# Moving two sets of transposes in the first group of a fused GFNet and GEGLU backward kernel

## The chip, the cores and the metric

The kernel runs on one core of a Trainium2 chip, in one launch. The metric is the device time of a run in microseconds; the median of several runs is given. A profile, taken by the hardware profiler on one further execution, shows every instruction of the five engines: TensorE (PE in the profile's rows, its weight loads PEld), VectorE (DVE), ScalarE (ACT), GpSimd (POOL) and SyncE (SP, which issues transfers here).

## What is computed

The forward pass mixes two branches with a gate; the kernel computes its output and the gradients of seven inputs. Cut to what matters:

```python
def _A_ref(x, w_r, w_i):                      # spectral branch
    X = rfft2(x) * (w_r + 1j * w_i)
    return irfft2(X, s=(S, D)).astype(bfloat16)

def _B_ref(x, w_gate, w_up, w_down):          # GEGLU branch
    return (gelu(x @ w_gate) * (x @ w_up)) @ w_down

x = A_x
g = sigmoid((x * gate_w).sum(-1, keepdims=True))
out = g * _A_ref(x, ...) + (1 - g) * _B_ref(x, ...)
_out, _vjp = jax.vjp(_f, A_x, A_w_r, A_w_i, B_w_gate, B_w_up, B_w_down, gate_w)
return (out, *_vjp(grad_out))
```

The sequence has S = 2048 rows, D = 576 columns, and the hidden width is 4608; tensors are bfloat16. Both branches take the same x.

## The kernel before

The 2048 rows are 16 tiles of 128 rows. The hidden width is cut into 18 groups of 256 columns (`for g in range(NG)`, L986), and each group is worked in four steps m = 0 to 3 of four row tiles each (L990). A step of the hidden layer consists of

- z, the product of the output gradient dO with the transposed down weights: 16 matmuls over four 128-column chunks (L413) and four over the 64-column tail (L418), written to one PSUM tile that ScalarE reads as da (L441);
- gate|up, the product of x with both other weights, in two halves of eight matmuls (L429), each into a PSUM tile of its own, with four tail matmuls ahead (L422). ScalarE reads each half three times: a copy xb and a copy hu (L450, L451) and a square q (L448);
- the element-wise part. `H_ew1` (L456 to L460) is four VectorE operations on the step's own tiles. `H_ew2` is a sigmoid on ScalarE (L476) and eight VectorE operations (L483 to L491), and it is held back by one step (`held`).

From group 1 on, weight gradients of the group before (L535, L553, L567) and pieces of the Fourier transforms are placed between the steps. After the last group a second phase reads the stored hidden gradients back and forms dx and the forward output (L1202).

The matmuls need x and dO with the model dimension on the partitions. The first group makes these transposed tensors, `xT` and `dOT`, on TensorE while it already works with them. `titems` (L370) yields three items for four row tiles: a first set of 8 transposes (chunks 0 and 1), a second set of 8 (chunks 2 and 3), and a third of 4 (the tails). Each item takes a PSUM tile, fills it with transposes (L378, tails L384) and copies it to `xT` or `dOT` (L385), on ScalarE (`AC`) or VectorE (`VC`) as the caller says.

In the first group the PSUM tiles of these items and of the gate's logits come from one pool, `pg`, with two buffers that are taken in turn. `gate(m + 1)` (L389) forms the logits of the next step's rows with 20 small matmuls (L394) and ScalarE reads them with a sigmoid (L396). `do2` are the three items of dO for step m + 2, copied by ScalarE, ScalarE and VectorE; `x1` are the three items of x for step m + 1, copied by ScalarE (VectorE at m = 0), VectorE and VectorE. Items in `rest` are handed to the next step's `H_mm` (L403), which runs them between z's chunks and z's tails (L414). Items in `early` run before the first half of gate|up, those in `mid_` between the first half and the held `H_ew2`, and those in `late_` inside the second half. Step 0 has an order of its own, and step 3 has no more items.

Each engine works its instructions in the order in which the program issues them, which is the order of the Python code here; no scheduler moves them. Where an instruction needs another engine's result, or a buffer that another engine still reads, it waits for a semaphore, and what is behind it on its engine waits too.

Of the kernel before, what the change touches and what calls it, by code (L numbers as in the profile page):

```python
# [255 lines left out]
def kernel(  # L256
# [176 lines left out]
    def ewt(tag, g):  # L433
        if tag in ("q", "s", "sg"):
            return unit([4, FG], name=tag) if g == 0 else ew.tile([P, 4, FG], BF16, tag=tag, name=tag, bufs=1)
        return ew.tile([P, 4, FG], BF16, tag=tag, name=tag, bufs=2)

    def H_da(g, m, z):
        da = ewt("da", g)
        for t in range(4):  # L440
            nc.scalar.activation(da[:, t, :], z[:, t % 2, t // 2, :], ACT.Copy, scale=omg32[:, 4 * m + t:4 * m + t + 1])  # L441
        return da
# [28 lines left out]
    def H_ew2(g, m, tiles, s, dH, da):  # L471
        xb, q, hu = tiles
        one = g < 2 or m == 2
        if one:
            om = xb
            nc.scalar.activation(s[:], s[:], ACT.Sigmoid, scale=2.0 * C_GELU)  # L476
        else:
            om, s = s, ewt("sg", g)
            nc.scalar.activation(s[:], om[:], ACT.Sigmoid, scale=2.0 * C_GELU)  # L479
            nc.scalar.activation(om[:], om[:], ACT.Sigmoid, scale=-2.0 * C_GELU)  # L480
        A = keepA.tile([P, 4, FG], BF16, tag="A", name="A")
        dHg, dHu = dH[:, :, 0, :], dH[:, :, 1, :]
        V.tensor_tensor(xb[:], xb[:], s[:], op=ALU.mult)  # L483
        V.tensor_tensor(dHu, da[:], xb[:], op=ALU.mult)
        V.tensor_tensor(A[:], xb[:], hu[:], op=ALU.mult)
        V.tensor_tensor(q[:], xb[:], q[:], op=ALU.mult)
        if one:
            V.tensor_scalar(om[:], s[:], -1.0, 1.0, op0=ALU.mult, op1=ALU.add)
        V.tensor_tensor(om[:], om[:], q[:], op=ALU.mult)  # L489
        V.tensor_tensor(om[:], om[:], s[:], op=ALU.add)  # L490
        V.tensor_tensor(dHg, dHg, om[:], op=ALU.mult)  # L491
        fsl = slice(g * FG, (g + 1) * FG)
        def store():
            for k, tl in ((0, A[:]), (2, dHu), (1, dHg)):
                LD.dma_start(scr[k][m][:, :, fsl].rearrange("t p f -> p t f"), tl)
        stores.append(store)
        kept.setdefault(g, []).append((A, dH))
# [453 lines left out]
    def want(pr):  # L951

        n0 = FIRST[-1]
        if pr < len(FIRST):
            return FIRST[pr]

        def load(n):

            return n + 0.5 * min(max(n - mid_at, 0), n_mid)
        share = load(n0) + (load(n_slots) - load(n0)) * (pr + 1 - len(FIRST)) / (LASTP - len(FIRST))  # L960
        n = n0
        while n < n_slots and load(n + 1) <= share + 1e-9:
            n += 1
        return int(min(n, n_slots) + 1e-9)
# [12 lines left out]
    carry, pend, held, rest = [], None, [], []  # L977
# [8 lines left out]
    for g in range(NG):  # L986
        if g == 1:
            pgs.close()
            pw = ps1.enter_context(tc.tile_pool(name="pw", bufs=2, space=PSUM, **kw))
        for m in range(NPR):  # L990
            pr = g * NPR + m
            n = want(pr) - done[0]
            done[0] += n
            hs = [h for u in pend[m] for h in u] if pend else []
            inside = pend[5].get(m, []) if pend else []

            def side_work(us):
                while side and us > 0:
                    us -= side[0][0]
                    side.pop(0)[1]()  # L1000
            tiles = [ewt(tag, g) for tag in ("xb", "q", "hu")]
            state = []

            def sigs(g=g, m=m, tiles=tiles, state=state):
                H_ew2(g, m, tiles, *state)
            if g == 0:
                def items(src, dst, t, *cp):
                    return titems(src, dst, 4 * t, (pgtile,) * 3, cp) if t < NPR else [None] * 3
                do1 = items(dB, dOT, 1, VC, VC, VC) if m == 0 else []
                do2 = items(dB, dOT, m + 2, AC, AC, VC)  # L1010
                x1 = items(xn, xT, m + 1, AC if m else VC, VC, VC)
                z, xy_full = H_mm(g, m, ([opening] if m == 0 else []) + rest)
                rest = []
                da = H_da(g, m, z)
                if m == 0:
                    early, mid_, late_ = do1[:2], [do1[2], x1[0]], x1[1:]
                elif m < NPR - 1:
                    early, mid_, late_ = x1[:2], x1[2:], []
                else:
                    early, mid_, late_ = [], [], []  # L1020
                for f in early:
                    f()
                xy = xy_full(0)
                for f in mid_:
                    f()
                if held:
                    held.pop()()
                for part in (1, 0):
                    H_act(0, xy, tiles, part)

                def between():
                    for f in late_:
                        f()
                xy = xy_full(1, between)
                for part in range(2):
                    H_act(1, xy, tiles, part)
                if m == 0:
                    build_R(nc, tb, unit, 4)
                    columns_B(nc, tb, res)
                elif m == 1:  # L1040
                    next(makeB)
                if m < NPR - 1:
                    gate(m + 1)
                else:
                    V.tensor_copy(g32[:], g_bf[:])
                    V.tensor_scalar(gs32[:], g32[:], SD2, None, op0=ALU.mult)
                if m + 2 < NPR:
                    do2[0]()
                    do2[1]()
                    rest = [do2[2]]  # L1050
                state += [*H_ew1(g, tiles, da), da]
                held.append(sigs)
            else:
                z, xy_full = H_mm(g, m)
                da = H_da(g, m, z)
                for f in inside:
                    f()
                xy = xy_full(0)
                if held:
                    scale_dB(0, AC)  # L1060
                    held.pop()()
                for part in (1, 0):
                    H_act(0, xy, tiles, part)
                k0 = int(n > 0 and pr > 7 and ready())
                xy = xy_full(1, fft_next if k0 else None)
                for part in range(2):
                    H_act(1, xy, tiles, part)
                state += [*H_ew1(g, tiles, da), da]
                if pr == 5:
                    scale_dB(1, AC)  # L1070
                    scale_dB(2, VC)
                    build_R(nc, tb, unit, 8)
                    build_R(nc, tb, unit, 12)
                elif pr == 6:
                    scale_dB(3, VC)
                    next(makeB)
                side_work(4.4)
                jobs = carry + hs
                total = sum(w for w, _ in jobs)
                at, k = 0.0, k0  # L1080
                tables = {6: 0}.get(pr)
                for i, (w, f) in enumerate(jobs):
                    if k < n and (at >= total * k / n - 0.45 or len(jobs) - i <= n - k):
                        fft_next()
                        k += 1
                    if i == tables:
                        run_late(tb)
                        wcopy[0] = VC
                    if pr == NG * NPR - 1 and at == 0.0:
                        sigs()  # L1090
                    f()
                    at += w
                wcopy[0] = AC
                while k < n:
                    fft_next()
                    k += 1
                flush()
                if pr == 6:
                    next(makeB)
                if pr < NG * NPR - 1:  # L1100
                    sigs()
            carry = []
            if m < 3 and g + 1 < NG:
                load_w(g + 1, m)
            if done[0] == n_slots or (pr >= wgT_from and pr % 2 == 0 and len(wgT_all) < 20):
                load_wgT()
                if done[0] == n_slots:
                    load_wgT()
        carry = pend[4] if pend else []
        pend = W_units(g)  # L1110
# [241 lines left out]
```

## Time and profile before

| | |
|---|---|
| median of 4 runs | 1409.44 us (1409.06 to 1410.46) |
| the profiled execution, its own time | 1409.15 us |
| span of the profile, first to last instruction | 1407.3 us |
| TensorE busy | 1384.6 us |
| VectorE, ScalarE, GpSimd busy | 748.7, 712.4, 246.1 us |
| granted TensorE clock over the span | 1.000 |

The span is cut into stages by the busy time of the engines. Columns are the stage in us, its length, and for each engine the busy time with the number of instructions, then the granted TensorE clock, the mean share of the transfer engines, and GB/s.

```profile
20.00:30.00 10.00, 9.32 (x107) 6.42 (x105) 7.15 (x22) 8.75 (x17) 5.27 (x20) 1.00 0.48 71
30.00:40.00 10.00, 8.47 (x99) 5.96 (x97) 7.80 (x15) 8.50 (x17) 0.00 (x0) 1.00 0.27 81
40.00:50.00 10.00, 9.76 (x88) 5.91 (x85) 9.43 (x18) 8.20 (x20) 0.00 (x0) 1.00 0.27 83
```

The engines are PE, PEld, DVE, ACT and POOL in this order. These thirty microseconds hold the steps 1 to 3 of the first group. Starts in the timelines are counted from the span's start. Matmuls overlap each other in the rows, so the distance from one row's start to the next tells better than a row's duration how long a set holds TensorE.

### The profile page before, as it was taken

What the parts mean: (1) busy time and instruction counts of PE and PEld (TensorE: products, weight loads), DVE (VectorE), ACT (ScalarE), POOL (GpSimd) and SP (SyncE); (2) the same over time, 40 slices, a digit from 0 to 9 for tenths busy, and PEclk for the clock granted to TensorE, in tenths of its full rate; (3) what the DMA queues carried; (4) which work ended last, traced back from release to release, by engine and by line L of the source; (5) the groups of instructions that cost most, each with busy time, mean ns of one, the idle gap of its engine ahead of it and who ended that gap; (6) DMA issues with size and microseconds to landing.
All of it is one profiled execution on the core that took longest, in us unless ns stands there. A gap on an engine that the chain in (4) does not pass through costs nothing.

```text
span 1407.3 us, 26025 instructions
## 1 busy us (share of the span) xinstructions
PE 1384.6 (98%) x10272; PEld 913.1 (65%) x10272; DVE 748.7 (53%) x1408; ACT 712.4 (51%) x1309; POOL 246.1 (17%) x486
## 2 busy tenths in 40 slices
PE   8999999999999999999999999999999999999999
PEld 6556566565565556566566566555777777777777
DVE  7875655655888777885666666561000642212101
ACT  6867767777778778767777776661000000000000
POOL 3000111123353633423101111110000100000000
PEclk9999999999999999999999999999999999999999
DMA  7423435345464655556456464849999998878874
GB/s 216 123 83 111 122 109 135 89 142 160 108 155 132 157 159 154 125 151 165 123 140 178 127 162 132 198 119 278 182 195 202 222 191 168 160 160 161 159 152 89
DMA packets 510647, 214.49 MB, mean 152 GB/s; under 512 B 312539, under 2 KB 503709, under 8 KB 510525
## 3 DMA queue, kind: packets, MB, share of 16 engines
q1 hardware_dynamic: 493402, 187.44, 57.0%
q0 software_dynamic: 14912, 24.24, 6.2%
q8 instruction: 80, 1.31, 0.4%
q10 hardware_dynamic: 2210, 1.15, 0.3%
q14 instruction: 43, 0.34, 0.1%
HBM read 41.05 MB, written 93.84 MB: 96 GB/s over the span
## 4 chain that ended last, share of the span: by engine, by line
PE 56%; ACT 1%; DMA 1%; SPq 1%; DVE 1%; issue 0%; ACTq 0%
PE acc L1202 30%; PE xy L429 7%; PE wps L553 7%; PE wps L535 4%; PE z L413 4%; PE wps L567 1%; DMA wd_all<-in_B_w_down_dram 1%; PE xy L422 1%; SPq L1127 1%; PE z L418 1%; PE pf L867 1%; PE pf L869 1%; ACT ZT L844 0%; PE pf L841 0%; ACT hu L451 0%
## 5 line engine op out<-in xcount | busy, mean ns | idle before, releaser
L1202 PEld LDWEIGHTS <-pin 128*128 128x128 bf16 x3456 | 338.0, 98 | 86.2 <-issue 0.9
L553 PE MATMUL wps<-dH,xn 128*128 128x512 bf16 x1152 | 270.8, 379 | 0.0
L429 PE MATMUL xy<-wgu,xT 128*128 128x512 bf16 x1152 | 270.3, 379 | 0.0
L429 PEld LDWEIGHTS <-xT 128*128 128x128 bf16 x1152 | 106.5, 98 | 133.0 <-issue 24.8
L553 PEld LDWEIGHTS <-xn 128*128 128x128 bf16 x1152 | 111.4, 98 | 118.4 <-issue 0.6
L1219 ACT COPY bo<-acc 128x288 f32<-128x288 f32 x32 | 12.7, 398 | 304.4 <-PE acc L1202 304.4
L535 PE MATMUL wps<-dB,A 128*128 128x288 bf16 x1152 | 154.2, 286 | 1.0 <-DVE dB L984 0.9
L560 POOL DMA_DIRECT2D out_dram<-dw x134 | 72.7, 546 | 445.3 <-ACT dw L504 419.5
L1202 PE MATMUL acc<-wgT,pin 128*128 128x288 bf16 x1152 | 143.9, 286 | 0.3 <-ACT dw L504 0.3
L1202 PE MATMUL acc<-wuT,pin 128*128 128x288 bf16 x1152 | 143.6, 286 | 0.0
L1202 PE MATMUL acc<-wd_all,pin 128*128 128x288 bf16 x1152 | 142.6, 286 | 0.0
L413 PE MATMUL z<-wdT,dOT 128*128 128x256 bf16 x1152 | 137.5, 272 | 3.9 <-ACT Xg L710 1.0
L535 PEld LDWEIGHTS <-A 128*128 128x128 bf16 x1152 | 112.1, 98 | 34.7 <-issue 1.9
L413 PEld LDWEIGHTS <-dOT 128*128 128x128 bf16 x1152 | 112.4, 98 | 27.0 <-issue 6.7
L441 ACT ACTIVATE da<-z,omg 128x256 bf16<-128x256 f32 x288 | 112.1, 472 | 17.5 <-PE z L418 16.7
L450 ACT CAST xb<-xy 128x512 bf16<-128x512 f32 x144 | 85.1, 591 | 48.8 <-PE xy L429 48.8
L1274 DVE SCALAR_TENSOR_TENSOR f32t<-gwf,dlog,b16t 128x576 f32<-128x576 f32 x16 | 13.1, 817 | 173.1 <-DMA b16t<-dxa_scr 173.1
L448 ACT ACTIVATE q<-xy 128x512 bf16<-128x512 f32 x144 | 87.6, 612 | 17.3 <-DVE xb L489 8.7
L483 DVE TENSOR_TENSOR xb<-xb,sg 128x1024 bf16<-128x1024 bf16 x48 | 33.2, 691 | 104.1 <-ACT sg L479 104.1
L451 ACT CAST hu<-xy 128x512 bf16<-128x512 f32 x144 | 87.5, 608 | 0.0
L504 ACT CAST dw<-wps 128x512 bf16<-128x512 f32 x72 | 42.2, 587 | 68.2 <-PE wps L553 58.4
L1233 DVE SCALAR_TENSOR_TENSOR b16t<-b16t,g,f32t 128x576 bf16<-128x576 bf16 x16 | 13.1, 818 | 95.3 <-DMA b16t<-a_scr 95.0
(216 smaller groups left out, 1653.3 us busy)
## 6 DMA issues: line engine op xcount, KB each, us to landing
scr<-dH SPq DMA_DIRECT2D x144, 256.0 KB, 3.4
scr<-A SPq DMA_DIRECT2D x72, 256.0 KB, 2.7
out_dram<-dw POOLq DMA_DIRECT2D x134, 64.0 KB, 2.4
wd_all<-in_B_w_down_dram SPq DMA_DIRECT2D x3, 1728.0 KB, 12.2
out_dram<-dwd POOLq DMA_DIRECT2D x34, 144.0 KB, 2.9
scr_p<-Vt SPq DMA_DIRECT2D x32, 145.0 KB, 2.8
wgu<-in_B_w_gate_dram SPq DMA_DIRECT2D x18, 256.0 KB, 4.0
wgu<-in_B_w_up_dram SPq DMA_DIRECT2D x18, 256.0 KB, 3.3
```

Of the source, the lines that this page charges most:

```text
L413: nc.tensor.matmul(zo(t), lhsT=dOT[:, ci, t, :], rhs=wdT[:, ci, :], start=(t % 4 < 2 and ci == 0), stop=False)
L429: nc.tensor.matmul(xy[k][:, t % 2, :], lhsT=xT[:, ci, t, :], rhs=wgu[:, ci, :], start=False, stop=(ci == 3))
L441: nc.scalar.activation(da[:, t, :], z[:, t % 2, t // 2, :], ACT.Copy, scale=omg32[:, 4 * m + t:4 * m + t + 1])
L448: nc.scalar.activation(q[:, h, :], xy[:, :, 0:FG], ACT.Square)
L450: nc.scalar.copy(xb[:, h, :], xy[:, :, 0:FG])
L451: nc.scalar.copy(hu[:, h, :], xy[:, :, FG:2 * FG])
L483: V.tensor_tensor(xb[:], xb[:], s[:], op=ALU.mult)
L504: wcopy[0](out, in_)
L535: nc.tensor.matmul(wps[:, :288], lhsT=tl(0, t)[:, fch * P:(fch + 1) * P], rhs=dB[:, t, h * 288:(h + 1) * 288], start=(t == 0), stop=(t == ...
L553: nc.tensor.matmul(wps[:].rearrange("p a b -> p (a b)"), lhsT=xn[:, t, c * P:(c + 1) * P], rhs=kt[t // 4][1][:, t % 4].rearrange("p k f -> ...
L560: wst[0].dma_start(ov[:, c, fsl], dw[:, k, :])
L1202: nc.tensor.matmul(acc[:, :288], lhsT=src[:, r, :], rhs=w_of(r)[:, h * 288:(h + 1) * 288], start=(first and r == 0), stop=(last and r == F ...
```

## The change

Two lists in the first group's branch are cut at another place. At m = 0 and 1 the second set of dO transposes for step m + 2 no longer runs at the end of the step; it goes into `rest` with the third, and so runs in the next step between z's chunks and z's tails. At m = 1 and 2 the second set of x transposes no longer runs before the first half of gate|up, but after it, with the third.

```diff
@@ -1015,7 +1015,7 @@
                 if m == 0:
                     early, mid_, late_ = do1[:2], [do1[2], x1[0]], x1[1:]
                 elif m < NPR - 1:
-                    early, mid_, late_ = x1[:2], x1[2:], []
+                    early, mid_, late_ = x1[:1], x1[1:], []
                 else:
                     early, mid_, late_ = [], [], []
                 for f in early:
@@ -1046,8 +1046,7 @@
                     V.tensor_scalar(gs32[:], g32[:], SD2, None, op0=ALU.mult)
                 if m + 2 < NPR:
                     do2[0]()
-                    do2[1]()
-                    rest = [do2[2]]
+                    rest = do2[1:]
                 state += [*H_ew1(g, tiles, da), da]
                 held.append(sigs)
             else:
```

## The prediction

> **What bounds the kernel now.** I read the page first, then the timelines of TensorE, ScalarE and VectorE from 20 to 60 us, where every moved instruction lies, then the waits of TensorE.
>
> ```profile
> PE 1384.6 (98%) x10272; PEld 913.1 (65%) x10272; DVE 748.7 (53%) x1408; ACT 712.4 (51%) x1309; POOL 246.1 (17%) x486
> PE   8999999999999999999999999999999999999999
> ```
>
> TensorE is busy for 98% of the span. Whatever shortens its own line of work, and is not taken back by a wait further on, shortens the kernel; and all that a reordering can win is the idle time of TensorE. Between 20 and 50 us it holds three such gaps, all inside the first group:
>
> ```profile
> 20.76 0.61 PE L378 MATMUL pf<-ident,dB 128*128 128x128 bf16 x8
> 22.05 0.61 PE L378 MATMUL pf<-ident,dB 128*128 128x128 bf16 x8 [0.68 <-ACT g_bf L396]
> 22.49 1.91 PE L413 MATMUL z<-wdT,dOT 128*128 128x256 bf16 x16
> 24.24 0.39 PE L384 MATMUL pf<-ident,dB 128*128 128x128 bf16 x4
> ...
> 26.22 1.89 PE L429 MATMUL xy<-wgu,xT 128*128 128x512 bf16 x8
> 27.95 0.39 PE L384 MATMUL pf<-ident,xn 128*128 128x128 bf16 x4
> ...
> 31.79 0.61 PE L378 MATMUL pf<-ident,dB 128*128 128x128 bf16 x8 [0.78 <-ACT g_bf L396]
> ...
> 35.05 0.62 PE L378 MATMUL pf<-ident,xn 128*128 128x128 bf16 x8
> 36.42 0.61 PE L378 MATMUL pf<-ident,xn 128*128 128x128 bf16 x8 [0.75 <-DVE dOT L385]
> ...
> 41.05 1.91 PE L413 MATMUL z<-wdT,dOT 128*128 128x256 bf16 x16
> ```
>
> The columns are start, duration, engine, line, tiles, count, and in brackets the idle time with what ended it. At 22.05 and 31.79 the second set of dO transposes waits for a PSUM buffer of the pool pg (two buffers, taken in turn), which the gate's logits hold until ScalarE's sigmoid (L396) has read them. z, 16 matmuls that need nothing of this, stands behind it. At 36.42 the second set of x transposes waits for the buffer of the third dO set, whose copy VectorE makes late. Why late:
>
> ```profile
> 28.37 0.42 DVE L385 COPY xT<-pf 128x512 bf16<-128x512 bf16 x1 [1.26 <-PE pf L384]
> 28.71 0.68 DVE L483 TENSOR_TENSOR xb<-xb,s 128x1024 bf16<-128x1024 bf16 x1
> ...
> 35.95 0.42 DVE L385 COPY dOT<-pf 128x512 bf16<-128x512 bf16 x1
> 37.07 0.69 DVE L385 COPY xT<-pf 128x1024 bf16<-128x1024 bf16 x1 [0.70 <-PE pf L378]
> 39.02 0.42 DVE L385 COPY xT<-pf 128x512 bf16<-128x512 bf16 x1 [1.26 <-PE pf L384]
> 39.36 0.68 DVE L483 TENSOR_TENSOR xb<-xb,s 128x1024 bf16<-128x1024 bf16 x1
> ```
>
> From 28.37 VectorE works without a gap to the copy at 35.95, and from 39.02 to 46.68. Each stretch starts when TensorE delivers the third x set (L384, 27.95 and 38.59). So a second line of work runs beside TensorE's: third x set, its copy, eight element-wise operations from L483 to L491, four from L456 to L460, next dO copy. It comes back to TensorE through ScalarE:
>
> ```profile
> 49.80 0.39 PE L422 MATMUL xy<-wgu,xT 64*128 64x512 bf16 x2 [0.24 <-ACT hu L451]
> ```
>
> **The change, step by step.** It adds and removes no instruction and no DMA: 8 dO transposes (second set) and 8 x transposes (second set) change place on TensorE, at m=0 to 1 and at m=1 to 2. ScalarE, VectorE, GpSimd and SyncE issue the same instructions in the same order, so no queue is passed there. The pg buffers are taken in the same turn too. I walk through with the spacing of the rows as durations: 8 transposes 0.44 (22.05 to 22.49), z 1.75 (22.49 to 24.24), third dO set 0.32, z's tails (L418) 0.23, gate|up's tails (L422) 0.52, half of gate|up 1.73 (26.22 to 27.95), third x set 0.22, gate 0.51; on ScalarE a copy of 1024 columns 1.03 (0.89 when one follows another), four da operations 1.44; a semaphore's hop about 0.05 (sigmoid ends 22.00, TensorE starts 22.05).
>
> First step. The first dO set ends its issue at 21.20. z now follows at once: its own wait is for the da of the step before, over at 16.93. z takes 21.20 to 22.95; the gate's buffer came free at 22.00, so the second dO set runs 22.95 to 23.39 without a wait. The third needs ScalarE's copy of the first (22.36 to 23.39): 23.44 to 23.76. Tails to 24.51. Then the first x set needs the copy of the second dO set, which is the new wait: the copy cannot start before 23.6 and ends at 24.63, so the x set starts at 24.68, 0.17 late, against 25.31. Queued behind it are the first half of gate|up and all of TensorE's later work; behind the later copy on ScalarE stand da (24.5, before 25.05) and the x copy (25.94, before 26.49), both still earlier. Half of gate|up 25.12 to 26.85, second and third x set to 27.52, other half to 29.24, gate to 29.75. Against 30.40 that is 0.65 won.
>
> VectorE meanwhile: the copy of the second x set ran at 26.42 in idle time that costs nothing (1.21 and 1.26 us idle on both sides). Now it starts at 27.53, between TensorE's delivery and L483. TensorE delivers the third set 0.65 earlier, but this copy (0.60 from one copy to the next, 0.34 from the short copy to L483) now lies in front of the third set's: the third copy is at 28.13 and L483 at 28.47 against 28.71. VectorE wins only 0.24.
>
> Second step. First dO set 29.75 to 30.19, z to 31.94, second set to 32.38 (the sigmoid, 0.65 earlier, ends at 31.09, so no wait), third set after ScalarE's copy (31.45 to 32.48) 32.53 to 32.85, tails to 33.60, first x set after the copy of the second dO set (32.6 to 33.63) 33.68 to 34.12, half of gate|up 34.12 to 35.85. Here the second x set needs VectorE's copy of the third dO set: 35.95 less 0.24 is 35.71, ends 36.13, so TensorE starts at 36.18. Of the wait of 0.93 that begins at 35.49 today, 0.33 is left, because 1.73 of matmuls now lie in front of it. Second and third x set to 36.84, other half to 38.57, gate to 39.08; z of m=3 starts there against 41.05, 1.97 won. VectorE gets the second x set at 36.85 (row: 37.07), the third at 37.45, L483 at 37.79 against 39.36: 1.57 won.
>
> Third step and after. VectorE and, through L457 and the sigmoid L476 (45.78), ScalarE keep 1.57. TensorE, 1.97 ahead, would start its second pair of L422 at 47.58, but the hu cast (ends 49.74) now ends at 48.17: the wait of 0.24 becomes 0.64, and TensorE too is down to 1.57. From there all three are 1.57 earlier, and the next meetings (weight gradients at 53.59 and 61.37, dH ready at 52.13 and 60.10) keep their distances. What could stand still, the transfers, does not matter: the last piece of the next group's wdT is issued by 29.04 and such a piece lands in 2.1, and z needs it at 45.1 at the earliest.
>
> Sum: 1.57 off the profiled span of 1407.3 gives 1405.7; the profiled execution took 1409.15, 1.85 more than its span, and gives 1407.6. The median of the runs shown is 0.29 above it: 1409.44 less 1.57 is 1407.9.
>
> The bounds of what the trace does not show. The new wait of the first x set: 0 at best, a whole copy (1.03) at worst; I take 0.17, since only the copy's end lies past TensorE's arrival. With the whole copy in the first step L483 comes 0.86 later than 28.47, the dO copy ends at 36.99, the second x set starts at 37.04 and L483 follows 1.61 later (as 37.79 follows 36.18) at 38.65: 0.7 is still won. Upwards, the wait at L422 may give nothing back, and 1.97 stays. So 0.7 to 1.97, and 1.57 by the rows.
>
> A rule speaks against the order. The Trainium skill, "TensorE: Matmul & The Clock Gate", Part 4, gives a 128x128 transpose about 275 ns in a kernel. By it the 8 transposes that now stand in front of VectorE's stretch would hold TensorE 2.2 us and not 0.44, L483 would come 1.76 later, and the sum would be a loss of about 0.2. The rows say 0.44 for eight, so it is not used.
>
> **The rivals.** First, the wait only moves: the gain stays on the early steps and a later meeting takes it. For it: VectorE has under 1 us of idle from 39 to 62, and from 50 to 130 TensorE meets ScalarE's copies often (3.4 idle from 80 to 130). Against it: these meetings are with engines that are themselves 1.57 ahead. It gives 1409.4.
>
> Second, the shift also loosens later waits: 1.97 kept, and the two longest of ScalarE's ve copies at 100.76 (0.79) and 109.93 (1.06) gone, 3.8 in all: 1405.6. For it: they are short waits that an earlier ScalarE would end. Against: TensorE is earlier by as much.
>
> Third, slower: TensorE's waits for ScalarE in the transform stage grow. These are the rows, with total, count and longest:
>
> ```profile
> PE pf L596 <- ACT ve L616: 1.8, 4, 1.1
> PE pf L705 <- ACT Xx L710: 1.8, 4, 0.8
> ...
> PE pf L705 <- ACT Xg L710: 1.3, 2, 0.6
> PE z L413 <- ACT Xg L710: 1.0, 2, 0.5
> ...
> PE z L413 <- ACT ve L616: 0.8, 1, 0.8
> ```
>
> They sum to 6.7 us. ScalarE's copies there share their place with stores and loads of the same buffers, whose landing (2.8 us for Vt) is not tied to TensorE's step. If a start 1.57 earlier meets them worse, each wait can lengthen: by half in all, +3.4 less 1.57 is 1411.3; doubled, 1414.6. It decides once these waits have grown by more than 1.57. Against it: ScalarE and SyncE are earlier by as much as TensorE, so the meetings should be the same.
>
> **How the numbers follow.** The forecast has 0.66, no gain 0.14, more 0.10, slower 0.10. A measurement of this kernel can tell about 0.2%, 2.8 us, from no change; the forecast is 0.11%, so faster and within it. Faster by more than that (under 1406.6): the second rival and 0.03 of the forecast, 0.13. Slower (over 1412.3, waits grown by 4.4 or more): 0.06 of the third rival. Between: 0.81. The range leaves out the second and third rival: 1406.6 to 1410.2, the runs' own spread of 0.7 on the no-gain case included.
>
> **What would show it.** In the profile after: no idle before the second dO set, z at 21.2 and about 30.2; an idle of 0.1 to 0.3 before the first x set of m=1 and 2; the second x set of m=2 waiting about 0.3 for VectorE; L483 at 28.5 and 37.8; z of m=3 at 39.1; the wait for hu at L422 grown to about 0.6; the same later rows some 1.6 earlier. It is wrong if the first x set starts after 25.5, or if rows at 53 us are early and rows past 600 us are not.

## The result and the profile after

The changed kernel takes 1407.68 us in the median of 33 runs (1407.0 to 1409.32); the kernel before, measured beside it, 1409.21 us in the median of 53 (1408.68 to 1410.84). The ratio is 0.9990, with a 95% interval of 0.9985 to 0.9994: 1.53 us faster, clear of noise and well inside 0.2%. The profiled execution took 1407.33 us with a span of 1405.4 us, against 1409.15 and 1407.3.

The waits of TensorE in the kernel after, with total, count and longest (the same view as in the prediction):

```profile
PE pf L705 <- ACT Xx L710: 1.8, 4, 0.8
PE pf L596 <- ACT ve L616: 1.8, 4, 1.1
...
PE pf L705 <- ACT Xg L710: 1.2, 2, 0.6
PE z L413 <- ACT Xg L710: 1.0, 2, 0.5
PE pf L378 <- ACT g_bf L396: 1.0, 1, 1.0
...
PE z L413 <- ACT ve L616: 0.8, 1, 0.8
PE xy L422 <- ACT hu L451: 0.6, 1, 0.6
```

Two of the three waits for the gate's sigmoid (2.4 us in all before) are gone; the one left belongs to step 0, which the change does not touch. The wait for the hu cast has grown from 0.24 to 0.61. The waits of the transform stage, 6.7 us in five rows before, are 6.6 us.

TensorE's timeline in the first group:

```profile
20.86 0.61 PE L378 MATMUL pf<-ident,dB 128*128 128x128 bf16 x8
21.31 1.91 PE L413 MATMUL z<-wdT,dOT 128*128 128x256 bf16 x16
23.05 0.61 PE L378 MATMUL pf<-ident,dB 128*128 128x128 bf16 x8
...
24.76 0.61 PE L378 MATMUL pf<-ident,xn 128*128 128x128 bf16 x8
25.21 1.89 PE L429 MATMUL xy<-wgu,xT 128*128 128x512 bf16 x8
...
30.28 1.91 PE L413 MATMUL z<-wdT,dOT 128*128 128x256 bf16 x16
...
36.23 0.61 PE L378 MATMUL pf<-ident,xn 128*128 128x128 bf16 x8 [0.16 <-DVE dOT L385]
...
39.13 1.91 PE L413 MATMUL z<-wdT,dOT 128*128 128x256 bf16 x16
...
48.25 0.39 PE L422 MATMUL xy<-wgu,xT 64*128 64x512 bf16 x2 [0.61 <-ACT hu L451]
```

z follows the first dO set at once (21.31 after 20.86), and the second dO set runs behind it without idle time in its row. The x set that now stands behind the late copy starts at 24.76. The second x set of m=2 still waits for VectorE, but for 0.16 and not 0.75. VectorE's timeline beside it:

```profile
27.58 1.02 DVE L385 COPY xT<-pf 128x1024 bf16<-128x1024 bf16 x2 [2.26 <-PE pf L378]
28.52 0.68 DVE L483 TENSOR_TENSOR xb<-xb,s 128x1024 bf16<-128x1024 bf16 x1
...
35.76 0.42 DVE L385 COPY dOT<-pf 128x512 bf16<-128x512 bf16 x1
36.87 1.02 DVE L385 COPY xT<-pf 128x1024 bf16<-128x1024 bf16 x2 [0.70 <-PE pf L378]
37.81 0.68 DVE L483 TENSOR_TENSOR xb<-xb,s 128x1024 bf16<-128x1024 bf16 x1
```

The copies of the second and third x set now stand together (x2) straight in front of L483. L483 comes 0.19 earlier in the first step and 1.55 in the second.

From there the lead is kept. The first weight-gradient matmul starts at 52.04 instead of 53.59 (1.55), a group of L535 in the middle at 594.67 instead of 596.30 (1.63), the second phase's first group at 977.53 instead of 979.16 (1.63), and the last operation of the chain at 1402.46 instead of 1404.28 (1.82).

### The profile page after: what moved, and what is told of

Same layout as the page of the kernel before. It is cut to its first block, busy times and chain, and to the rows that moved or that the text cites. A ratio compares the mean times of both kernels' runs of the same rounds, so it can differ in the third digit from the quotient of the medians.

```text
span 1405.4 us, 26025 instructions
## 1 busy us (share of the span) xinstructions
PE 1385.0 (99%) x10272; PEld 913.8 (65%) x10272; DVE 748.5 (53%) x1408; ACT 712.3 (51%) x1309; POOL 245.8 (17%) x486
## 3 DMA queue, kind: packets, MB, share of 16 engines
HBM read 41.05 MB, written 93.84 MB: 96 GB/s over the span
## 4 chain that ended last, share of the span: by engine, by line
PE 56%; ACT 1%; DMA 1%; SPq 1%; DVE 1%; issue 0%; ACTq 0%
PE acc L1201 30%; PE xy L429 7%; PE wps L553 7%; PE wps L535 4%; PE z L413 4%; PE wps L567 1%; DMA wd_all<-in_B_w_down_dram 1%; PE xy L422 1%; SPq L1126 1%; PE z L418 1%; PE pf L867 1%; PE pf L869 1%; ACT ZT L844 0%; PE pf L841 0%; ACT hu L451 0%
## 5 line engine op out<-in xcount | busy, mean ns | idle before, releaser
L553 PE MATMUL wps<-dH,xn 128*128 128x512 bf16 x1152 | 270.8, 379 | 0.0
L553 PEld LDWEIGHTS <-xn 128*128 128x128 bf16 x1152 | 111.5, 98 | 118.4 <-issue 0.6
L535 PE MATMUL wps<-dB,A 128*128 128x288 bf16 x1152 | 154.2, 286 | 1.0 <-DVE dB L984 0.9
L535 PEld LDWEIGHTS <-A 128*128 128x128 bf16 x1152 | 112.1, 98 | 34.7 <-issue 1.9
L483 DVE TENSOR_TENSOR xb<-xb,sg 128x1024 bf16<-128x1024 bf16 x48 | 33.2, 691 | 104.2 <-ACT sg L479 104.1
```

Of the source, the lines that this page charges most:

```text
L535: nc.tensor.matmul(wps[:, :288], lhsT=tl(0, t)[:, fch * P:(fch + 1) * P], rhs=dB[:, t, h * 288:(h + 1) * 288], start=(t == 0), stop=(t == ...
L553: nc.tensor.matmul(wps[:].rearrange("p a b -> p (a b)"), lhsT=xn[:, t, c * P:(c + 1) * P], rhs=kt[t // 4][1][:, t % 4].rearrange("p k f -> ...
```

## The experiments

The moved instructions all lie in one stretch, so each kernel is read at two marks of its profile, both counted from the start of the first dO set of step 0: the first weight-gradient matmul of group 1 (L553), and z of the eighth step (88.28 in the kernel before). They are free of what varies between executions before and after the stretch. The medians and ratios were taken beside runs of the kernel before, whose median was 1409.21 for the kernel after, 1409.70 for e1 to e4 and 1409.77 for e5 to e8. Each mark comes from a single profile. The kernel after and e8 do the same work up to L553 and reach it at 31.18 and 31.17, e6 and e7 both at 30.44, so the first mark repeats to about 0.01.

| kernel | L553 | z, eighth step | median us | ratio, 95% interval |
|---|---|---|---|---|
| before | 32.83 | 67.52 | | |
| after | 31.18 | 65.86 | 1407.68 | 0.9990 [0.9985, 0.9994] |
| e1, dO part alone | 32.31 | 67.00 | 1409.37 | 0.9997 [0.9988, 1.0006] |
| e2, x part alone | 32.30 | 66.99 | 1409.34 | 0.9998 [0.9990, 1.0007] |
| e3, x moved at m=2 only | 31.01 | 65.69 | 1408.11 | 0.9989 [0.9980, 0.9997] |
| e4, x moved at m=1 only | 32.54 | 67.23 | 1410.32 | 1.0002 [0.9994, 1.0011] |
| e5, casts first | 30.61 | 65.61 | 1407.82 | 0.9991 [0.9982, 0.9999] |
| e6, e3 and e5 | 30.44 | 65.46 | 1407.58 | 0.9984 [0.9975, 0.9993] |
| e7, e6 and e8 | 30.44 | 64.34 | 1406.75 | 0.9980 [0.9971, 0.9989] |
| e8, dB scaling moved | 31.17 | 64.75 | 1406.74 | 0.9981 [0.9972, 0.9990] |

**The dO part alone**, on the kernel before:

```diff
                     do2[0]()
-                    do2[1]()
-                    rest = [do2[2]]
+                    rest = do2[1:]
```

> Only the dO part: the second dO set goes into the next step's z; the x sets stay as before. The measure is the distance from the first dO set of step 0 (20.76 before, 20.86 after) to the first weight-gradient matmul of group 1 (L553, 53.59 and 52.04): 32.83 us before, 31.18 after. My theory, two lines of work (TensorE's, and VectorE's from the third x set's copy on) that must both come earlier: the stalls at the sigmoid go, but TensorE now arrives earlier at the second x set of m=2, which still waits for VectorE's copy of the third dO set; that wait grows from 0.75 to about 1.5, L483 of the second step stands at 38.9, and only 0.5 is won: distance 32.35, time about 0.5 under the kernel before. The rival, each stall is worth its own length and parts add up: 0.68 and 0.78 are won, distance 31.4, time 1.5 under.

Measured 32.31, so 0.52 won where both stalls at the sigmoid are gone. What takes the rest, in TensorE's timeline of e1:

```profile
34.05 0.61 PE L378 MATMUL pf<-ident,xn 128*128 128x128 bf16 x8
36.17 0.61 PE L378 MATMUL pf<-ident,xn 128*128 128x128 bf16 x8 [1.51 <-DVE dOT L385]
```

TensorE reaches the second x set early and waits 1.51 us for VectorE's dO copy, twice as long as before. The two stalls were not worth their length.

**The x part alone**, on the kernel before:

```diff
-                    early, mid_, late_ = x1[:2], x1[2:], []
+                    early, mid_, late_ = x1[:1], x1[1:], []
```

> Only the x part: at m=1 and 2 the second x set goes behind the first half of gate|up; the dO sets stay as before. Two lines: both stalls at the sigmoid (0.68, 0.78) stay; in the first step VectorE's copy of the second x set now delays L483 from 28.7 to 29.1; in the second step the wait for the dO copy goes, TensorE wins 0.93, but L483 comes at 38.8 instead of 39.36, so 0.5 is left after the wait at L422: distance 32.3, time about 0.5 under. So the two parts alone would sum to 1.0 where both together gave 1.55. The rival, parts add: the x part is what is left of the whole after the two stalls, about 0.1, distance 32.7.

Measured 32.30, 0.53 won. In TensorE's timeline of e2 both stalls at the sigmoid are still there, and the wait for hu is as long as in the kernel after, although less is won:

```profile
23.63 0.61 PE L378 MATMUL pf<-ident,dB 128*128 128x128 bf16 x8 [0.68 <-ACT g_bf L396]
...
33.37 0.61 PE L378 MATMUL pf<-ident,dB 128*128 128x128 bf16 x8 [0.78 <-ACT g_bf L396]
...
50.85 0.39 PE L422 MATMUL xy<-wgu,xT 64*128 64x512 bf16 x2 [0.62 <-ACT hu L451]
```

The parts alone win 0.52 and 0.53, both together 1.65. The dO part brings TensorE early to a place where only the x part has work for it; and the x part alone delays VectorE in the first step (L483 stands 8.33 us after the first dO set in e2, 7.95 in the kernel before), which only the dO part makes up for (7.66 in the kernel after). That parts add up is refuted at the marks; the medians, 0.33 and 0.36 under the kernel before with intervals across 1, cannot tell either from no change.

**The x part at one step only**, on the kernel after; e3 first, then e4:

```diff
-                    early, mid_, late_ = x1[:1], x1[1:], []
+                    early, mid_, late_ = x1[:3 - m], x1[3 - m:], []
```

```diff
-                    early, mid_, late_ = x1[:1], x1[1:], []
+                    early, mid_, late_ = x1[:m], x1[m:], []
```

> The kernel after, but the second x set moves only at m=2; at m=1 it stays before the first half of gate|up. Two lines: in the first step VectorE's copy lies in idle time again, L483 at about 28.25 instead of 28.5; the dO copy of the second step comes 0.25 earlier, the second x set of m=2 no longer waits, L483 of the second step at about 37.6 instead of 37.8: 0.2 better than the kernel after, distance 30.95 to 31.0. The rival: each moved set helps; the one left at m=1 costs something or nothing, distance 31.2 or more.

> The kernel after, but the second x set moves only at m=1; at m=2 it stays before the first half of gate|up. Two lines: the move at m=1 delays VectorE (its copy in front of L483) and at m=2 TensorE waits for VectorE's dO copy with nothing in front, about 1.9 us; L483 of the second step at about 39.1, only 0.2 won: distance 32.6, less won than with the dO part alone. The rival, parts add: both sigmoid stalls gone, 1.4 won, distance 31.4.

Measured 31.01 for e3 and 32.54 for e4, both as the two lines of work say. In e3 TensorE's second x set of m=2 has no wait at all; in e4 it has the longest of all kernels (the timelines of e3 and e4):

```profile
36.06 0.61 PE L378 MATMUL pf<-ident,xn 128*128 128x128 bf16 x8
```

```profile
36.69 0.61 PE L378 MATMUL pf<-ident,xn 128*128 128x128 bf16 x8 [1.89 <-DVE dOT L385]
```

So of the two moves of an x set, the one at m=2 carries the gain, and the one at m=1 costs 0.17 (31.18 less 31.01): it puts VectorE's copy in front of L483, where it was in idle time before. In the medians this cost is not shown: e3 is 1.59 under the kernel before and the kernel after 1.53.

**The casts before the sigmoid**, on the kernel after. It asks whether it is VectorE, through the held sigmoid, that takes part of TensorE's lead back at L422:

```diff
+                if m == NPR - 1:
+                    H_act(0, xy, tiles, 1)
                 if held:
                     held.pop()()
-                for part in (1, 0):
+                for part in (0,) if m == NPR - 1 else (1, 0):
                     H_act(0, xy, tiles, part)
```

> The kernel after, and at m=3 of the first group ScalarE makes the casts xb and hu of the first half of gate|up before the held sigmoid L476 (which waits 1.21 us for VectorE), not behind it. It asks whether VectorE, through that sigmoid, is what takes 0.4 of TensorE's 1.97 back at L422. Two lines: the wait of 0.61 for hu at L422 goes, L553 starts 30.6 us after the first dO set instead of 31.18; VectorE's L483 of m=2 is 0.4 later. But VectorE has only 0.4 us of idle from there to 77, so the dB scaling (L984) is not earlier, TensorE's wait there grows from 0.95 to about 1.5, and z of the eighth step is reached as in the kernel after: 65.9 us after the first dO set (before: 67.5). Time as the kernel after. The rival, a wait that goes is won for good: 65.25 there, 0.6 under the kernel after.

The rows of the kernel after that it starts from, of ScalarE, VectorE and TensorE:

```profile
44.23 1.06 ACT L476 ACTIVATE s<-s 128x1024 bf16<-128x1024 bf16 x1 [1.21 <-DVE s L457]
...
53.29 0.69 DVE L483 TENSOR_TENSOR xb<-xb,s 128x1024 bf16<-128x1024 bf16 x1 [0.35 <-ACT s L476]
...
77.22 0.43 DVE L456 TENSOR_SCALAR s<-q 128x1024 bf16<-128x1024 bf16 x1 [0.40 <-ACT q L448]
...
77.14 1.63 PE L535 MATMUL wps<-dB,A 128*128 128x288 bf16 x12
79.72 7.17 PE L535 MATMUL wps<-dB,A 128*128 128x288 bf16 x52 [0.95 <-DVE dB L984]
```

The wait at L422 is gone, and L553 starts at 30.61, as expected. Two rows of ScalarE's timeline in e5, and TensorE's next wait there:

```profile
44.02 0.59 ACT L450 CAST xb<-xy 128x512 bf16<-128x512 f32 x1 [0.64 <-PE xy L429]
...
44.97 1.07 ACT L476 ACTIVATE s<-s 128x1024 bf16<-128x1024 bf16 x1
```

```profile
79.83 4.35 PE L535 MATMUL wps<-dB,A 128*128 128x288 bf16 x29 [1.27 <-DVE dB L984]
```

The wait for dB grows from 0.95 to 1.27, and at z of the eighth step only 0.25 of the 0.57 is left. I had expected nothing left; the miss is VectorE's idle time. Besides the 0.40 that I counted before its row at 77.22, the 0.35 of idle before L483 at 53.29 in the kernel after is 0.19 here, so VectorE could give up 0.56 against the 0.40 by which e5 delays it (its L483 of m=2 starts 24.86 after the first dO set, 24.46 in the kernel after). That accounts for 0.16 of the 0.25; the other 0.09 is in no idle time that the view lists. That a wait which goes is won for good is refuted too.

**e6** is e3 and e5 together:

> e3 (x sets moved only at m=2) and the casts of e5. Two lines: L553 at 30.4, but z of the eighth step at 65.7 as in e3 (65.69), the wait for dB taking back what the casts win. The rival: 65.1.

Measured 30.44 and 65.46: again 0.23 kept of the casts' 0.57, as in e5 and not nothing.

**The dB scaling moved**: the last quarter of dB is scaled by ScalarE in the fifth step, in idle time, and no longer by VectorE in the seventh. e8 is the kernel after with this alone, e7 is e6 with it:

```diff
+                if pr == 4:
+                    scale_dB(3, AC)
                 if pr == 5:
                     scale_dB(1, AC)
...
                 elif pr == 6:
-                    scale_dB(3, VC)
                     next(makeB)
```

> e6, and the scaling of the last quarter of dB moved from VectorE in the seventh step to ScalarE in the fifth, where ScalarE is idle for 3.5 us (56.2 to 59.7 in the kernel after) and four scalings take 2.8. Two lines: now the last wait of this stretch (0.95) goes as well and the casts' 0.6 is kept: z of the eighth step at about 64.1, 3.4 less than in the kernel before and 1.7 less than after; time about 1406.0 to 1406.5 where the kernel before has 1409.4. The rival: the scaling on ScalarE delays da or the casts behind it, and TensorE gets a new wait of about 1; 65.

> The kernel after with that scaling moved alone. Two lines: the wait of 0.95 goes, z of the eighth step at 64.9, 0.95 less than after; time about 0.9 under the kernel after. The rival: something else is late right behind it and the wait moves, 65.9.

e8 reaches z of the eighth step at 64.75, 1.11 earlier than the kernel after where 0.95 was expected. The profile counts idle time from a matmul's modelled end; from the last one's issue (77.14 and twelve times 0.1225, the spacing of 16 in 1.96) the wait for dB that ended at 79.72 was 1.11 long. e7 is at 64.34 where 64.1 was expected, 0.41 ahead of e8: with the wait for dB gone, more than half of what the casts and e3 win (0.57 and 0.17) is kept. TensorE's next wait, in e7:

```profile
82.80 4.08 PE L535 MATMUL wps<-dB,A 128*128 128x288 bf16 x32 [0.80 <-DVE dwd L504]
```

It is longer than e8's at the same place (0.47). The 0.33 more is what is missing between 0.41 and the 0.74 of both, so by this row VectorE again takes the rest back. Both kernels are 3.0 us under the kernel before in the median, clear of noise, and at the mark 1.52 and 1.11 ahead of the kernel after. Their medians (1406.75 and 1406.74) can't tell which of the two is faster. The time expected for e7 was 1406.0 to 1406.5, so 1406.75 misses it by 0.25.

## Why the prediction was right

The forecast was 1.57 us and 1407.9; measured were 1.53 between the medians and 1407.68. Allowing for the start, which was 0.10 later in the profile of after, the steps came out so:

- The two stalls at the sigmoid go: yes. z at 21.31 (21.20 and 0.10 expected), second dO set at 23.05 (22.95), z of the second step at 30.28 (30.19).
- The new wait behind the late copy of the second dO set is short: yes. The first x set started at 24.76 (24.68). By the spacing of starts it is 0.17 late in the first step and 0.07 in the second; the prediction's steps had 0.17 and 0.08, but its list of signs asked for 0.1 to 0.3 in both, which the second does not meet. The third dO set started 0.03 late (23.52 after a set that ends its issue at 23.49).
- VectorE wins little in the first step, since the second x set's copy now stands in front of L483: yes, 0.19 by the clock of the profile and 0.29 counted from the start, 0.24 expected. e3 shows the cost: without it L483 stands at 28.30 and 0.17 more is won in the end.
- TensorE wins 1.97 up to z of m=3, VectorE 1.57 up to L483: 39.13 against 41.05, 1.92 and with the start's 0.10 2.02; 37.81 against 39.36, 1.55 and 1.65. VectorE's gain was some 0.08 larger than expected. The second x set of m=2 still waits for VectorE, 0.16 by the view and 0.32 by the spacing of starts (34.18, 1.73 of matmuls, 36.23); 0.33 was expected.
- The wait at L422 takes the difference back: 0.61, expected 0.64. e5 takes this wait away and shows that its cause is VectorE's line through the held sigmoid.
- Later meetings keep their distances: yes, but for small sums. The wait for dB is the same, 0.94 and 0.95; between 52 and 594 us the lead grows from 1.55 to 1.63, and at the change of phase to 1.81 (979.24 instead of 981.05 in the chain). There the chain runs through SyncE's issues and the load of wd_all, and this load starts 1.81 earlier (965.51 instead of 967.32). TensorE's wait for ScalarE's dw copy, which stands behind it, is listed with 0.3 to 0.5 in six of the ten profiles and not in after, e1, e5 and e7, which does not follow the marks; so the last 0.18 is not shown to come from the change.

That the median came within 0.04 of the forecast is partly luck. The interval leaves 0.85 to 2.1 us, and the profiles give other numbers for the same change: 1.65 at L553, counted from the first dO set, and 1.9 in the span. The prediction also held that only about 0.2%, 2.8 us, can be told from no change; with 33 and 53 runs 1.53 us could.

The rivals. That a later meeting takes all of it was wrong for this change, but it is what happens to a little over half of the casts' gain in e5, two steps further on. The prediction counted 3.4 us of idle between 80 and 130 us as meetings with ScalarE's copies; 0.94 of it is this wait for VectorE's dB. That later waits loosen as well was wrong: the two ve waits named for it are still 0.8 and 1.1. That the transform stage's waits grow was wrong: 6.7 and 6.6 us.

The Trainium skill's figure of about 275 ns for a transpose ("TensorE: Matmul & The Clock Gate", Part 4) is not the time for which a transpose holds TensorE in these sets: eight take 0.45 us in the kernel after (24.76 to 25.21), and with that the sum came out.

## What to carry to other kernels

A stall on the busiest engine is worth its length only if the engine that it meets next comes earlier too; here two stalls of 0.68 and 0.78 were worth 0.52 alone and 1.65 with a second move. So follow both lines of work up to where they next wait for each other, and price a move by the later of the two. A copy that is moved out of idle time and in front of a long run of work costs there, and what that run releases is the place to look for the end of the gain.

## What had not been expected

TensorE's clock dips in some executions, and this is a large part of what varies between runs. Two profiles, of e2 and e7, caught it, both before the moved instructions. In the view by stages of e2 the granted clock is 0.60 from 15 to 19 us (columns: stage, length, PE, PEld, DVE, ACT and POOL busy, clock, transfer share, GB/s), while the kernel before has 1.00 there:

```profile
15.00:19.00 4.00, 4.00 (x22) 2.11 (x22) 2.19 (x6) 1.97 (x7) 0.00 (x0) 0.60 1.05 389
```

```profile
15.00:19.00 4.00, 4.00 (x39) 2.59 (x39) 3.33 (x8) 3.44 (x9) 0.00 (x0) 1.00 1.08 363
```

In e2 the eight matmuls of half of gate|up that start at 15.70 take until 18.67, 2.97 us, where the kernel before needs 1.73 (15.36 to 17.09), and the first dO set starts at 22.34 instead of 20.76. e7's profile has the same dip (22.38). Of the 34 executions on record of the kernel after (the 33 of its median and one more), seven have a mean granted clock of 0.999 and take 1408.92 us in the median; the other 27 take 1407.61. The dip costs 1.3 us, nearly as much as the change wins, and falls on the stretch where TensorE still waits often (five waits up to 15 us).

The dip is also the likely reason why e4's median is above that of the kernel before although its second mark is 0.29 ahead: five of its eleven executions have a mean clock of 0.999, against four of the 33 beside them. Without all such executions the medians are under the kernel before by 0.59 (e1), 0.49 (e2), 1.53 (e3), 0.07 (e4), 2.11 (e5), 2.13 (e6), 3.01 (e7) and 2.87 (e8); the second marks are ahead by 0.52, 0.53, 1.83, 0.29, 1.91, 2.06, 3.18 and 2.77. This sorting was done afterwards and has no intervals, but it follows the marks to about 0.3.

The Trainium skill, "TensorE: Matmul & The Clock Gate", Part 1, says that the clock is halved after an idle window of about 3.4 us and that these windows run free of the kernel. The halved rate agrees with the trace: the granted clock in e2 is 0.50 from 15 to 18 us. That only some executions are hit would fit windows that run free. But no idle time of that length is in the rows: after the first matmul, the longest wait of TensorE before the dip in e2 is 0.97. What sets the dip off is not shown, and no run here was made to take it away.
